# Signs of the first head by an extra matmul instead of DMA, a new order of the first block, and the mix of some pairs in a later slot

## The chip, the cores and the metric

The kernel runs on one core of a Trainium2 chip. The metric is the time of one execution on the device in microseconds; the median of three runs of the kernel before is 281.64 us (281.24 to 282.11). A profiled execution gives a page and a trace, in which times count from the start of its span. The engines are named as in the profile: PE is TensorE (matmuls; PEld its weight loads), DVE VectorE, ACT ScalarE, POOL GpSimd, SP SyncE. SPq, ACTq and POOLq stand for an engine that issues a DMA.

## The reference

Two networks follow each other. The first is an attention in which query and key only see each other when the signs of six projections agree:

```python
q_bits = (np.einsum('bhsd,dk->bhsk', q, proj) > 0).astype(np.int64)
k_bits = (np.einsum('bhsd,dk->bhsk', k, proj) > 0).astype(np.int64)
q_bucket = np.sum(q_bits * powers, axis=-1)      # k_bucket likewise
mask = q_bucket[:, :, :, None] == k_bucket[:, :, None, :]
scores = np.where(mask, scale * np.matmul(q, k.transpose(0, 1, 3, 2)), -1000000000.0)
attn = softmax(scores)
out = np.matmul(attn, v)                         # (4, 8, 768, 64)
```

Its heads side by side are x (4, 768, 512) of the second, a channel mix, where x_prev is x shifted by one position of the sequence:

```python
xk = mu_k * x + (1.0 - mu_k) * x_prev
xr = mu_r * x + (1.0 - mu_r) * x_prev
k = np.maximum(xk @ w_k, 0.0)                    # 512 -> 1024
v = k * k @ w_v                                  # 1024 -> 512
r = 1.0 / (1.0 + np.exp(-(xr @ w_r)))
return r * v
```

There are 4 batches, 8 heads of 64 columns, 768 positions.

## The kernel before

Work goes by **pairs** of heads: 16 pairs, four to a batch, numbered n; the head within a pair is j. One pair has 12 **slots**, one for each head and each block of 128 keys (jc). The loop over all 192 slots (G) writes out the order of every engine by hand; engines work through their own queues in that order and wait for each other by semaphores.

In one slot: `score` (L319) multiplies a block of keys with all queries into one of two PSUM buffers (tag `sc`), and ScalarE takes the exponential (L332). Two slots later `pv` (L340) multiplies the result with the values into `oo`, one PSUM bank for the head. After a head's last block VectorE takes reciprocals (`rc`, L363) and writes the scaled head to `ob` (L364). For pairs 0 to 3 the two heads of a pair use banks A and C in turn; from pair 4 on both use bank A, since C and D then serve the channel mix.

What a pair needs beforehand:

- `load_qk`, `load_v`: loads of q, k and v, on SP, for the first pairs on GpSimd's queue as well.
- `turn` (L263): three transposes on TensorE turn q or k of one head; VectorE copies the result out of PSUM (`tq` L272, `tk` L274) and casts one half to bfloat16 into `aq` or `ak` (L278), GpSimd casts the other half (L277).
- `bits` (L281): the signs. A matmul with the projection (L287), a comparison on VectorE that gives +0.5 or -0.5 (`sg`, L291), and for each head and side two DMAs (L297), which put the six sign rows below the 64 rows of `aq` and `ak`. A score is then one matmul over 70 rows: equal signs add 1.5, and the exponential with its scale of 256 and bias of -384 makes everything else vanish.
- `values` (L302): the values and their sums in bfloat16, all on GpSimd.

After a pair, in slot 3 of the next, `turn_out` (L371) transposes `ob` back and writes `xt`, x of the second network. The first 127 columns, x_prev across a boundary, are copied by GpSimd (L384), for the last pair of a batch by VectorE. In slot 4 `mix` (L389) subtracts (`df`, L394), multiplies (L398) and adds (L405) on VectorE: this is xk. A second part gives xr later, in slot 8 as a rule.

The matmuls of the channel mix of a batch (`kp`, `rp`, `vp`, all recorded at L424) start in slot 5 of the next batch's first pair, spread evenly over four pairs in a queue of small items. `kr` and `k` are the squared relu (L447 on ScalarE or L449 on VectorE, L455 on VectorE).

Weights come during the first pairs: `load_w` by GpSimd's queue, `load_wv` (L542) by SP into one of two staging buffers, which GpSimd casts eight slots after the issue (L550); `weights` (L587) names the slots. The DMAs that SP issues take turns on eight semaphores, so an issue waits until the one eight places ahead has landed.

Before the loop the kernel does all of pair 0's turns and signs and half of pair 1's turns.

Of the kernel before, what the change touches and what calls it, by code (L numbers as in the profile page):

```python
# [9 lines left out]
FP32 = mybir.dt.float32  # L10
BF16 = mybir.dt.bfloat16
INT32 = mybir.dt.int32
AF = mybir.ActivationFunctionType
ALU = mybir.AluOpType
AX = mybir.AxisListType

P = 128
# [12 lines left out]
def kernel(  # L30
# [13 lines left out]
    nc = tc.nc  # L44
# [123 lines left out]
    def fast():  # L168
        with ExitStack() as fx:
# [12 lines left out]
            obp = pool("ob", 2)  # L182
            rcp = pool("rc", 4)
            xtp = pool("xt", 1)
            stg = pool("stg", 2)
            aug = pool("aug", 1)
            dfp = pool("df", 1)
            mixp = pool("mix", 2)
# [74 lines left out]
            def turn(n, i, j, which):  # L263
                side = "qk"[i]
                au = augs[n % NSET]
                tp = bank(which, [P, HALF], FP32, f"tp{side}{n}_{j}")
                for c in range(3):
                    cols = slice(c * P, (c + 1) * P)
                    nc.tensor.transpose(tp[:, cols], nats[n][:, i, j, cols], ident32)  # L269
                dst = t32p.tile([P, HALF], FP32, name=f"t{side}{n}_{j}", tag=f"t{side}{j}")  # L270
                if side == "q":
                    nc.vector.tensor_copy(dst, tp)  # L272
                else:
                    nc.vector.tensor_scalar(  # L274
                        out=dst, in0=tp, scalar1=ALPHA, scalar2=None, op0=ALU.mult
                    )
                nc.gpsimd.tensor_copy(au[side, j][0:D, 0:HALF], dst[0:D, :])  # L277
                nc.vector.tensor_copy(au[side, j][0:D, HALF:S], dst[D:P, :])  # L278
                t32s[n, side, j] = dst

            def bits(n, js, which, two_queues=False):  # L281
                au = augs[n % NSET]
                groups = [(side, j) for j in js for side in "qk"]
                ng = len(groups)
                bb = bank(which, [32 * ng, HALF], FP32, f"bb{n}_{js[0]}")
                for g, key in enumerate(groups):
                    nc.tensor.matmul(  # L287
                        bb[32 * g : 32 * g + 32, :], projp, t32s[(n,) + key], start=True, stop=True
                    )
                sg = sgp.tile([32 * ng, HALF], BF16, name=f"sg{n}_{js[0]}", tag="sg")  # L290
                nc.vector.tensor_scalar(  # L291
                    out=sg, in0=bb, scalar1=0.0, scalar2=0.5, op0=ALU.is_gt, op1=ALU.subtract
                )
                for g, key in enumerate(groups):
                    eng = nc.scalar if two_queues and key[0] == "k" else nc.sync
                    for e in range(2):
                        eng.dma_start(  # L297
                            out=au[key][D:AUG, e * HALF : (e + 1) * HALF],
                            in_=sg[32 * g + NB * e : 32 * g + NB * e + NB, :],
                        )  # L300

            def values(n, j):  # L302
                vf = vfs[n][:, j, :]
# [15 lines left out]
            def score(n, j, jc):  # L319
                au = augs[n % NSET]  # L320
                pt = ptp.tile([P, S], BF16, name=f"pt{n}_{j}_{jc}", tag="pt")
                pts[n, j, jc] = pt
                sc = scp.tile([P, 2, 512], FP32, name=f"sc{n}_{j}_{jc}", tag="sc")
                for sp in range(2):
                    nc.tensor.matmul(  # L325
                        sc[:, sp, 0:HALF],
                        au["k", j][:, jc * P : (jc + 1) * P],
                        au["q", j][:, sp * HALF : (sp + 1) * HALF],
                        start=True,
                        stop=True,  # L330
                    )
                nc.scalar.activation(  # L332
                    pt.rearrange("p (s q) -> p s q", s=2),
                    sc[:, :, 0:HALF],
                    AF.Exp,
                    bias=expb,
                    scale=SCALE,
                )
# [203 lines left out]
            def load_wv(c0):  # L542
                st = stg.tile([P, 2, DM], FP32, name=f"wvs{c0}", tag="stg")
                nc.sync.dma_start(
                    out=st,
                    in_=moe_w_v[c0 * P : (c0 + 2) * P, :].rearrange("(c p) f -> p c f", p=P),
                )
                later(
                    8,
                    lambda: nc.gpsimd.tensor_scalar(  # L550
                        out=wv_sb[:, c0 : c0 + 2, :], in0=st, scalar1=0.5, scalar2=1.0,
                        op0=ALU.mult, op1=ALU.mult,
                    ),
                )
# [9 lines left out]
            for _ in range(22):  # L564
                nc.tensor.matmul(idle, epsm, epsm, start=True, stop=True)
            turn(0, 0, 0, "B")
            turn(0, 1, 0, "D")
            bits(0, (0,), "A", two_queues=True)
            load_qk(2, eng=nc.gpsimd)
            turn(0, 0, 1, "B")  # L570
            turn(0, 1, 1, "D")
            bits(0, (1,), "C")
            load_v(1)
            nc.sync.dma_start(
                out=mu_rows[0:NDC, :], in_=moe_mu_k.rearrange("(c p) -> c p", p=P)
            )
            nc.sync.dma_start(
                out=mu_rows[NDC : 2 * NDC, :], in_=moe_mu_r.rearrange("(c p) -> c p", p=P)
            )
            values(0, 0)  # L580
            turn(1, 0, 0, "B")
            turn(1, 1, 0, "D")
            values(0, 1)

            weights = {  # L587
# [3 lines left out]
            }  # L591
            LAG = 2
            MIXSLOT = 6
# [11 lines left out]
            for G in range(nslots + LAG):  # L605
                clock[0] = G
                n, s = divmod(G, 12)
                live = G < nslots
                run_due()

                if live and s == (5 if n == 0 else 3):
                    if n + 3 < NPAIRS:
                        load_qk(n + 3)
                    if n + 2 < NPAIRS:
                        load_v(n + 2)
                w = weights.get(n, {}).get(s)
                if w:
                    if w[0] == "v":
                        load_wv(w[1])
                    else:  # L620
                        load_w(*w)
                old = chunks[G - LAG] if G >= LAG else None
                first = old is not None and old[2] == 0
                if live:
                    score(*chunks[G])
                if old and not first:
                    pv(*old, oo_bank(*old[:2]))
                rate = 25.9 / (NPB * 12 + (3 if n >= NPAIRS - NPB else 0))
                ffn(rate / 2)
                mb = misc_bank(n, s)  # L630
                if live:
                    if n == 0:
                        if s in (0, 1):
                            turn(1, s, 1, "BD"[s])
                    if n == 1 and s == 0:
                        mups = bank(mb, [P, 2 * NDC], FP32, "mups")
                        nc.tensor.transpose(mups, mu_rows, ident32[0 : 2 * NDC, 0 : 2 * NDC])
                        nc.vector.tensor_copy(mu_sb, mups)
                    if s == (3 if n == 0 else 1) and n + 1 < NPAIRS:
                        bits(n + 1, (0, 1), mb)  # L640
                    if s == 3 and n >= 1:
                        turn_out(n - 1, mb)
                    if s == 4 and n >= 1:
                        mix((n - 1) // NPB, (n - 1) % NPB, 0)

                    if n in (NPB, NPB + 1) and G - NPB * 12 in (7, 9, 11, 13):
                        mix(0, (G - NPB * 12 - 7) // 2, 1)
                    if n > NPB and s == 8:
                        mix((n - 1) // NPB, (n - 1) % NPB, 1)
                    if s in (5, 7, 9, 11) and n + 2 < NPAIRS:  # L650
                        x = (s - 5) // 2
                        turn(n + 2, x % 2, x // 2, mb)
                    if s in (6, 10) and n + 1 < NPAIRS:
                        values(n + 1, s // 10)
                    if s in (8, 10) and NKEEP <= n + 1 < NPAIRS:
                        norm(n + 1, (s - 8) // 2)
                ffn(rate / 2)
                if old and first:
                    pv(*old, oo_bank(*old[:2]))
                if live and n >= NPB and n % NPB == 0 and s == MIXSLOT - 1:  # L660
                    queue.extend(ffn_items(n // NPB - 1))
# [213 lines left out]
```

## Time and profile before

| what | value |
|---|---|
| median of three runs | 281.64 us |
| profiled execution | 281.45 us |
| its span | 279.6 us |
| TensorE busy | 262.2 us (94%) |
| ScalarE busy | 215.0 us (77%) |
| VectorE busy | 198.6 us (71%) |
| GpSimd busy | 113.3 us (41%) |
| exponentials, 192 of them | 166.5 us |
| first exponential starts | 12.94 us |

The page's chain of work that ended last is followed back from the last instruction: each step is what the next one waited for. In a timeline, a line has the start, the length (of a merged group: from first start to last end), engine, line of the kernel, operation, and output and input by name; what stands in brackets is how long the engine stood idle before it and what it waited for.

### The profile page before, as it was taken

How to read it: one execution, taken by the hardware profiler on the slowest of the kernel's cores; microseconds unless marked ns; L12 is line 12 of the kernel's file. 1: busy time of each engine (PE TensorE's matmuls, PEld its weight loads, DVE VectorE, ACT ScalarE, POOL GpSimd, SP SyncE). 2: the span in 40 equal slices, each digit the busy share in tenths (PEclk: the TensorE clock that was granted, in tenths of full speed). 3: DMA queues.
4: the chain of work that ended last, by engine and by line, in shares of the span. 5: the costliest groups of instructions: out<-in, count | busy, mean ns of one | idle time of the engine just before them, and what ended most of it. 6: DMA issues, size and time to landing. Idle time of an engine off the chain costs nothing.

```text
span 279.6 us, 6894 instructions
## 1 busy us (share of the span) xinstructions
PE 262.2 (94%) x2530; PEld 165.4 (59%) x2561; DVE 198.6 (71%) x438; ACT 215.0 (77%) x318; POOL 113.3 (41%) x300
## 2 busy tenths in 40 slices
PE   7999997899999999999999999999999889989991
PEld 5466765666565665656565765656565556545540
DVE  3766839879997866769698766769698835576541
ACT  2199995898799896878989896878998898449800
POOL 5885667665554350714455260715444600000000
PEclk9999997999999999999999999999999999999997
DMA  7459597253213050726122040815220001320042
GB/s 231 167 115 208 179 328 248 43 173 101 77 59 117 6 172 4 218 110 191 59 69 108 14 164 7 272 53 166 84 60 4 5 2 39 114 76 2 0 151 86
DMA packets 19896, 29.95 MB, mean 107 GB/s; under 512 B 2184, under 2 KB 15056, under 8 KB 19856
## 3 DMA queue, kind: packets, MB, share of 16 engines
q1 hardware_dynamic: 17928, 25.89, 27.9%
q0 software_dynamic: 1536, 3.15, 5.3%
q8 instruction: 22, 0.36, 0.5%
q10 hardware_dynamic: 392, 0.40, 0.5%
q14 instruction: 18, 0.15, 0.2%
HBM read 24.12 MB, written 6.29 MB: 109 GB/s over the span
## 4 chain that ended last, share of the span: by engine, by line
PE 66%; ACT 9%; DVE 8%; DMA 7%; issue 3%; SPq 3%; POOL 2%; ACTq 0%; DVEq 0%
PE sc L325 15%; PE vp L424 13%; PE kp L424 12%; PE oo L352 8%; ACT pt L332 6%; PE rp L424 5%; DMA wvs<-in_moe_w_v_dram 4%; PE bb L287 4%; PE tpq L269 3%; PE tpk L269 2%; SPq L297 2%; PE ot L378 2%; ACT sq L256 2%; PE oo L343 1%; DMA aq<-sg 1%
## 5 line engine op out<-in xcount | busy, mean ns | idle before, releaser
L332 ACT ACTIVATE pt<-sc,expb 128x768 bf16<-128x768 f32 x192 | 166.5, 904 | 39.4 <-PE sc L325 38.1
L325 PE MATMUL sc<-aq,ak 70*128 70x384 bf16 x384 | 94.9, 328 | 3.2 <-ACT pt L332 0.8
L352 PEld LDWEIGHTS <-pt 128*128 128x128 bf16 x1152 | 61.1, 98 | 26.6 <-issue 0.8
L352 PE MATMUL oo<-va,pt 128*128 128x65 bf16 x1152 | 66.9, 194 | 0.0
L424 PE MATMUL kp<-xk,wk_sb 128*128 128x384 bf16 x256 | 57.7, 325 | 0.8 <-DVE os L487 0.8
L325 PEld LDWEIGHTS <-ak 70*128 70x128 bf16 x384 | 34.9, 98 | 29.3 <-issue 9.1
L424 PE MATMUL vp<-wv_sb,k 128*128 128x512 bf16 (+1 forms) x186 | 50.3, 370 | 0.4 <-issue 0.2
L277 POOL CAST aq<-tq 64x384 bf16<-64x384 f32 x32 | 21.1, 658 | 63.3 <-DVE tq L272 63.3
L455 DVE TENSOR_TENSOR k<-kr 128x384 bf16<-128x384 bf16 x64 | 29.0, 459 | 15.5 <-ACT kr L447 14.3
L424 PEld LDWEIGHTS <-wk_sb 128*128 128x128 bf16 x256 | 22.2, 97 | 13.3 <-issue 4.2
L256 ACT ACTIVATE sq<-qk 128x768 bf16<-128x768 f32 x32 | 27.1, 847 | 0.1
L424 PE MATMUL rp<-wr_sb,xr 128*128 128x512 bf16 x79 | 24.9, 379 | 1.2 <-DVE kr L449 0.8
L424 PEld LDWEIGHTS <-k 128*128 128x128 bf16 x200 | 17.5, 97 | 12.0 <-issue 2.7
L447 ACT ACTIVATE kr<-kp 128x384 bf16<-128x384 f32 x36 | 17.7, 491 | 7.4 <-PE kp L424 7.4
L487 DVE SCALAR_TENSOR_TENSOR os<-th,vp 128x512 f32<-128x512 bf16 (+1 forms) x25 | 16.5, 663 | 9.0 <-PE vp L424 8.9
L384 POOL COPY xt<-xt 128x127 bf16<-128x127 bf16 x12 | 3.6, 302 | 46.4 <-DVE xt L379 46.4
L311 POOL TENSOR_TENSOR s<-vf 128x192 f32<-128x192 f32 x32 | 20.8, 650 | 0.0
L277 POOL CAST ak<-tk 64x384 bf16<-64x384 f32 x32 | 19.3, 602 | 2.4 <-DVE tk L274 2.4
L274 DVE TENSOR_SCALAR tk<-tpk 128x384 f32<-128x384 f32 x32 | 17.6, 550 | 3.4 <-PE tpk L269 3.3
L272 DVE COPY tq<-tpq 128x384 f32<-128x384 f32 x32 | 17.7, 552 | 2.1 <-PE tpq L269 2.0
L269 PE MATMUL tpq<-ident,qk 128*128 128x128 f32 x96 | 16.9, 287 | 2.4 <-DVE tq L272 1.7
L379 DVE COPY xt<-ot 128x768 bf16<-128x768 bf16 x16 | 8.9, 558 | 14.3 <-PE ot L378 14.2
(60 smaller groups left out, 320.0 us busy)
## 6 DMA issues: line engine op xcount, KB each, us to landing
vf<-in_v_dram SPq DMA_DIRECT2D x16, 384.0 KB
out_dram<-os SPq DMA_DIRECT2D x23, 256.0 KB
qk<-in_q_dram SPq DMA_DIRECT2D x13, 384.0 KB
qk<-in_k_dram SPq DMA_DIRECT2D x13, 384.0 KB
wvs<-in_moe_w_v_dram SPq DMA_DIRECT2D x4, 512.0 KB
aq<-sg SPq DMA_DIRECT2D x64, 4.5 KB
wk_sb<-in_moe_w_k_dram POOLq DMA_DIRECT2D x2, 512.0 KB, 5.4
ak<-sg SPq DMA_DIRECT2D x62, 4.5 KB
```

The costliest lines, as they stand in the source:

```text
L256: nc.scalar.activation(junk, nats[n][:, i].rearrange("p j f -> p (j f)"), AF.Square, accum_out=nrm[:, i, n : n + 1],)
L269: nc.tensor.transpose(tp[:, cols], nats[n][:, i, j, cols], ident32)
L272: nc.vector.tensor_copy(dst, tp)
L274: nc.vector.tensor_scalar(out=dst, in0=tp, scalar1=ALPHA, scalar2=None, op0=ALU.mult)
L277: nc.gpsimd.tensor_copy(au[side, j][0:D, 0:HALF], dst[0:D, :])
L311: nc.gpsimd.tensor_add(s3, vf[:, 0 : 3 * D], vf[:, 3 * D : 6 * D])
L325: nc.tensor.matmul(sc[:, sp, 0:HALF], au["k", j][:, jc * P : (jc + 1) * P], au["q", j][:, sp * HALF : (sp + 1) * HALF], start=True, stop=True,
L332: nc.scalar.activation(pt.rearrange("p (s q) -> p s q", s=2), sc[:, :, 0:HALF], AF.Exp, bias=expb, scale=SCALE,)
L352: nc.tensor.matmul(oo[:, ic, :], pts[n, j, jc][:, ic * P : (ic + 1) * P], vas[n, j][:, jc, :], start=False, stop=(jc == NC_ - 1 and ic == ...
L424: nc.tensor.matmul(box["t"], lhs(), rhs(), start=(i == 0), stop=(i == len(mms) - 1))
L447: nc.scalar.activation(kr, kp, AF.Relu)
L455: 1, lambda: nc.vector.tensor_tensor(out=k2, in0=kr, in1=kr, op=ALU.mult)
```

## The change

The first head's signs (pair 0, j = 0) no longer go into the sign rows of `aq` and `ak`. `first_signs` projects each half of its q and k by a matmul of 64 rows, compares, and leaves six rows of signs at partition 0. For this head a score is two matmuls that add up in PSUM: one over 64 rows of `ak` and `aq`, one over six rows of signs.

The order of the first block is another: before the loop stand the first head's turns and signs, its values, the load of pair 2 and head 1's q. Head 1's k and signs, its values, `load_v(1)`, the mu rows and all four turns of pair 1 move into slots 0 to 3; pair 1's signs move from slot 3 to slot 4, the loads of pair 3 from slot 5 to 6, and pair 2's turns to slots 7, 9, 10 and 11. The DMAs with head 1's k signs are issued by GpSimd.

There is one staging buffer instead of two, the cast follows ten slots after the load, and the slots of the weight loads change. `mix` for xk goes from slot 4 to slot 6, save after the last pair of a batch.

```diff
-            stg = pool("stg", 2)
+            stg = pool("stg", 1)
...
-                    eng = nc.scalar if two_queues and key[0] == "k" else nc.sync
+                    eng = nc.gpsimd if two_queues and key[0] == "k" else nc.sync
...
+            def first_signs():
+
+                res = []
+                for side in "qk":
+                    bb = scp.tile([NB, 2, 512], FP32, name=f"fb{side}", tag="sc")
+                    for e in range(2):
+                        nc.tensor.matmul(
+                            bb[:, e, 0:HALF],
+                            projp[e * D : (e + 1) * D, e * NB : (e + 1) * NB],
+                            t32s[0, side, 0][e * D : (e + 1) * D, :],
+                            start=True,
+                            stop=True,
+                        )
+                    sg = consts.tile([NB, 2, HALF], BF16, name=f"fs{side}")
+                    for es in (slice(0, 2),) if side == "q" else (slice(0, 1), slice(1, 2)):
+                        nc.vector.tensor_scalar(
+                            out=sg[:, es, :], in0=bb[:, es, 0:HALF], scalar1=0.0, scalar2=0.5,
+                            op0=ALU.is_gt, op1=ALU.subtract,
+                        )
+                    res.append(sg)
+                return res
...
+                own = n == 0 and j == 0
+                rows = slice(0, D if own else AUG)
                 for sp in range(2):
                     nc.tensor.matmul(
                         sc[:, sp, 0:HALF],
-                        au["k", j][:, jc * P : (jc + 1) * P],
-                        au["q", j][:, sp * HALF : (sp + 1) * HALF],
+                        au["k", j][rows, jc * P : (jc + 1) * P],
+                        au["q", j][rows, sp * HALF : (sp + 1) * HALF],
                         start=True,
-                        stop=True,
+                        stop=not own,
                     )
+                if own:
+                    sq, sk = (x.rearrange("p e q -> p (e q)") for x in signs0)
+                    for sp in range(2):
+                        nc.tensor.matmul(
+                            sc[:, sp, 0:HALF],
+                            sk[:, jc * P : (jc + 1) * P],
+                            sq[:, sp * HALF : (sp + 1) * HALF],
+                            start=False,
+                            stop=True,
+                        )
...
-                    8,
+                    10,
                     lambda: nc.gpsimd.tensor_scalar(
...
-            bits(0, (0,), "A", two_queues=True)
+            signs0 = first_signs()
+            values(0, 0)
             load_qk(2, eng=nc.gpsimd)
             turn(0, 0, 1, "B")
-            turn(0, 1, 1, "D")
-            bits(0, (1,), "C")
...
-            values(0, 0)
-            turn(1, 0, 0, "B")
-            turn(1, 1, 0, "D")
-            values(0, 1)
...
-                1: {0: ("v", 0), 2: ("v", 2), 10: ("r", 0, 2)},
-                2: {0: ("v", 4), 2: ("v", 6), 10: ("r", 2, 2)},
+                1: {0: ("v", 0), 6: ("r", 0, 2), 10: ("v", 2)},
+                2: {4: ("r", 2, 2), 8: ("v", 4)},
+                3: {6: ("v", 6)},
...
-                if live and s == (5 if n == 0 else 3):
+                if live and s == (6 if n == 0 else 3):
...
-                        if s in (0, 1):
-                            turn(1, s, 1, "BD"[s])
+                        if s == 0:
+                            turn(0, 1, 1, "D")
+                        if s == 1:
+                            bits(0, (1,), "C", two_queues=True)
+                            values(0, 1)
+                            load_v(1)
...
+                            turn(1, 0, 0, "B")
+                        if s == 2:
+                            turn(1, 1, 0, "D")
+                        if s == 3:
+                            turn(1, 0, 1, "B")
+                            turn(1, 1, 1, "D")
...
-                    if s == (3 if n == 0 else 1) and n + 1 < NPAIRS:
+                    if s == (4 if n == 0 else 1) and n + 1 < NPAIRS:
                         bits(n + 1, (0, 1), mb)
...
-                    if s == 4 and n >= 1:
+                    if n >= 1 and s == (4 if n % NPB == 0 else 6):
                         mix((n - 1) // NPB, (n - 1) % NPB, 0)
...
-                    if s in (5, 7, 9, 11) and n + 2 < NPAIRS:
-                        x = (s - 5) // 2
-                        turn(n + 2, x % 2, x // 2, mb)
+                    ts = (7, 9, 10, 11) if n == 0 else (5, 7, 9, 11)
+                    if s in ts and n + 2 < NPAIRS:
+                        x = ts.index(s)
+                        turn(n + 2, x % 2, x // 2, "BD"[x % 2] if n < NPB else mb)
```

More of the change, by code (lines that the diff above doesn't have):

```diff
@@ L567, in fast @@
             turn(0, 1, 0, "D")
-            bits(0, (0,), "A", two_queues=True)
+            signs0 = first_signs()
+            values(0, 0)
             load_qk(2, eng=nc.gpsimd)
             turn(0, 0, 1, "B")
-            turn(0, 1, 1, "D")
-            bits(0, (1,), "C")
[L573 to L579, printed above, removed]
-            values(0, 0)
-            turn(1, 0, 0, "B")
-            turn(1, 1, 0, "D")
-            values(0, 1)
             weights = {
                 0: {2: ("k", 0, 2), 8: ("k", 2, 2)},
[2 rows of a table removed]
[3 rows of a table added]
             }
@@ L632, in fast @@
                     if n == 0:
-                        if s in (0, 1):
-                            turn(1, s, 1, "BD"[s])
+                        if s == 0:
[4 more added lines that the diff above has]
+                            load_v(1)
+                            for i, mu in enumerate((moe_mu_k, moe_mu_r)):
+                                nc.sync.dma_start(
+                                    out=mu_rows[i * NDC : (i + 1) * NDC, :],
+                                    in_=mu.rearrange("(c p) -> c p", p=P),
+                                )
+                            turn(1, 0, 0, "B")
[4 more added lines that the diff above has]
+                            turn(1, 1, 1, "D")
                     if n == 1 and s == 0:
```

## The prediction

> **What bounds the kernel now.** I read the page first, then the chain of work that ended last for the first 62 us, the timelines of single engines there, and last the timeline of one pair in the stretch where the second network's matmuls run.
>
> ```profile
> PE 262.2 (94%) x2530; PEld 165.4 (59%) x2561; DVE 198.6 (71%) x438; ACT 215.0 (77%) x318; POOL 113.3 (41%) x300
> ...
> PE 66%; ACT 9%; DVE 8%; DMA 7%; issue 3%; SPq 3%; POOL 2%; ACTq 0%; DVEq 0%
> ```
>
> TensorE is the bound over the whole, but not in the first 62 us, where no channel-mix matmul runs yet: there ScalarE's exponentials follow each other at 0.79 us (eight in 6.47 us) and TensorE has little slack. The chain there:
>
> ```profile
> 8.55 3.81 DMA aq<-sg
> ...
> 12.41 0.49 PE sc L325 x2
> ...
> 32.70 4.00 DMA wvs<-in_moe_w_v_dram
> ...
> 36.78 1.04 POOL wv_sb L550
> ...
> 40.96 0.24 POOL xt L384
> ...
> 41.23 0.57 DVE df L394
> ```
>
> The first score waits for the first head's signs, which travel by DMA from 8.55 to 12.36. Later GpSimd stands in front of a weight that has not landed, so its shift of `xt` comes at 40.96 and VectorE, whose next instruction is the mix, stands 3.52 us. TensorE then waits for `tq`, queued behind that mix, and its granted clock falls:
>
> ```profile
> 43.36 0.55 PE L269 MATMUL tpq<-ident,qk 128*128 128x128 f32 x3 [1.75 <-DVE tq L272]
> ```
>
> ```profile
> 43.40:47.40 4.00, 4.00 (x32) 2.95 (x33) 3.77 (x9) 2.24 (x3) 3.84 (x9) 0.59 0.99 320
> ```
>
> The numbers before the last two are the granted clock (0.59) and, after it, DMA share and GB/s. From pair 4 on, one pair takes about 15.5 us and TensorE is dense. What matters there is bank A, which holds `oo` of both heads in turn: the second head's first `oo` matmul (L343) can't start before `ob` of the first has been read out by VectorE. Pair 5:
>
> ```profile
> 77.88 0.56 DVE L394 TENSOR_TENSOR df<-xt 128x768 bf16<-128x768 bf16 x1 [0.18 <-POOL xt L384]
> ...
> 78.72 0.49 PE L269 MATMUL tpq<-ident,qk 128*128 128x128 f32 x3
> ...
> 79.40 0.55 DVE L272 COPY tq<-tpq 128x384 f32<-128x384 f32 x1
> ...
> 80.27 0.55 DVE L449 TENSOR_SCALAR kr<-kp 128x384 bf16<-128x384 f32 x1
> ...
> 81.66 0.56 DVE L364 TENSOR_TENSOR ob<-oo,rc 128x384 bf16<-128x384 f32 x1
> ...
> 82.73 0.33 PE L343 MATMUL oo<-vs,epsm 128*128 128x390 bf16 x1
> ```
>
> The reader is to see two things: the mix (77.88 to 79.40) fills time in which VectorE has nothing else, since `tpq` ends at 79.21; and `ob` ends at 82.22, 0.5 us before TensorE needs the bank. In pair 13 there is no margin at all:
>
> ```profile
> 207.70 0.33 PE L343 MATMUL oo<-vs,epsm 128*128 128x390 bf16 x1 [0.21 <-DVE ob L364]
> ```
>
> **Part 1, the first block.** Removed: four DMAs for the first head's signs (two on SP, two on ACT; ACT was idle there). Added: four small fp32 matmuls, one 6x768 and two 6x384 comparisons, and two more matmuls of 384 columns in each of slots 0 to 5. Moved behind the first score: the turns of head 1's k and of pair 1, and head 1's signs; before, all but two of these turns lay in the shadow of the DMA.
>
> Walk. `tq` is ready at 5.54. A pass of 384 fp32 columns costs 0.64 cold (the bb matmul of 5.60). The two halves sit in different row groups; side by side, q takes 5.60 to 6.88 and k to 8.16. That row groups run side by side isn't in the trace; four column groups do (L287 at 15.28 to 15.30). In series it would cost 2.56 us more cold, about 1.65 since the clock is full from 10. The turn of head 1's q follows, 8.3 to 8.95. VectorE's comparisons cost 0.55 per 384 columns (L291), 768 columns between 0.56 (L379) and 1.1; either is done by 8.25, and k's first by 8.95. So the first score starts at 9.0 and its exponential at about 10.35 instead of 12.94.
>
> From 9.0 to the score of slot 6 TensorE has: score pair of slot 0, cold 0.64; its signs 0.33; five scores with signs at 0.66, 3.3; five turns at 0.33, 1.65; two signs groups at 0.75, 1.5; one opening of `oo` and four groups of pv, 0.95; and 18 changes of tile shape (128 rows, 64, 32, back).
>
> ```profile
> 15.30 0.51 PE L287 MATMUL bb<-tk,projp 128*32 128x384 f32 x1
> ...
> 15.65 0.49 PE L287 MATMUL bb<-tk,projp 128*32 128x384 f32 x1
> ...
> 16.07 0.50 PE L325 MATMUL sc<-aq,ak 70*128 70x384 bf16 x2
> ```
>
> The only change of shape in the trace is at L287: the second pass starts at 15.65 and takes 0.33 (15.30 to 15.63), the score follows at 16.07, so 0.09 is left. I take 0.1, together 1.8; the ends are 0 and 0.16 (a 384-column record lasts 0.33 and they start 0.165 apart), together 2.9. Sum 10.2: slot 6 at 19.2, its exponential, after that of slot 5 at 19.15, at 19.95. Before it was at 18.19 (16.61 plus two of 0.79). So the early start is used up by six slots of about 1.5 us on TensorE: +1.75, I take +1.6 (some passes overlap). Ends: 0 (no cost of switching, then ScalarE bounds) and +3.3 (row groups in series).
>
> The Trainium skill speaks against this part: "TensorEngine Tiling (Array Packing)", section Key Properties, has a change of tiling mode drain the engine. The trace shows 0.09 at L287, less than a full drain; with a drain of 0.16 at all 18 the sum would be about 1.1 us worse.
>
> Covers: head 1's q signs stay on SP, k signs take two issues on GpSimd (0.72 each by L238) behind `values(0,0)` (2.0), which waits for v (landed by 9.1 at the latest: issue 1.67, longest landing 7.4), `load_qk(2)` (1.45) and two casts (1.3): issued by about 15.2, landed 3.8 later by 8.55 to 12.36, 19.0 against slot 6 at 19.2. `load_qk(2)` goes out 4 us later; 6.2 to landing gives 18.7 against its turn in slot 7 at 20. Pair 1's signs go out at 18.3 instead of 16.2, eight SP issues of 0.7, as before about six us ahead of slot 12. `load_v(1)` and the two mu rows follow two SP issues; they have 5 us and more. Pair 2's turns move to slots 7, 9, 10 and 11, two slots ahead of their signs. Pair 3's loads go out behind pair 1's signs, at 24.5 instead of 22.48; its first turn, in slot 17, comes at about 28.8 (28.14 before), so the thinnest cover shrinks from 5.7 to 4.3. If one cover fails it costs 1 to 2, inside the upper end.
>
> **Part 2, pairs 1 to 4.** Weights are loaded further apart, cast ten slots after their issue, and the mix moves to slot 6, two slots behind GpSimd's shift. From slot 12 (23.27) to slot 53 (62.46 starts its exponential) lie 39.2 us where 40 exponentials need 31.6. Of the 7.6 left, four signs groups keep 0.55 each. The mix of pair 1 (0.48 at 28.7) and the great stall with its cold clock (42.47 to 51.6: 1.86 + 0.76 + 0.5 + 0.67 idle, less one signs group, plus 0.4 in slower exponentials) go: 0.5 + 3.5 = 4.0. The two wr loads (0.77 of GpSimd each) move up by 4 and 6 slots; their first matmul is at 76.67. Ends -3.0 and -4.4 (the rest is spread in hundredths). What is late next is the signs group. The one stage buffer makes SP wait for GpSimd's cast, with the next pair's eight sign DMAs behind it; they are needed 11 slots (9 us) later, which hides a cast that is up to 3 us late.
>
> **Part 3, pairs 5 and up.** VectorE's order in the built program is now xt, k, tq, aq, kr, df, xk, xk, k, rc, ob. `tq` can't start before 79.25 in pair 5. Start to start: tq 0.59, aq until kp is there (80.27), kr 0.57, df 0.59, xk 0.46, xk 0.47, k 0.4, rc 0.22, ob 0.56: 83.5 against 82.22 before, and the `oo` matmul goes from 82.73 to 83.7. Same working, with each pair's own tpq and kp: pair 6 +1.0 (tpq 94.70, oo was 98.21), 9 +0.8 (kr goes ahead of tq; oo was 145.61), 13 +0.75, 14 +0.8 (it has no turns; the two k and kr come first), 10 about 0 (no kr in between). Pairs 7, 11 and 15 have no kr and k there: 3.2 of VectorE in 3.6, no wait. 4, 8, 12 keep slot 4. Sum +4.3. The waits of VectorE for GpSimd go too:
>
> ```profile
> DVE df L394 <- POOL xt L384: 6.9, 10, 3.5
> ```
>
> That is 6.9 us in ten waits; the two of pairs 1 and 2 (0.39 and 3.52) lie in part 2, the eight here are 3.0 in all, and I count nothing for them, since they lie ahead of `tpq`'s end and TensorE waited for none of them. Ends +2.0 (half of the stalls fall on waits that are there anyway, like the 0.21 above) and +5.5.
>
> **Sum.** +1.6 - 4.0 + 4.3 = +1.9 on the profiled execution's 281.45 (span 279.6 and 1.85 around it): 283.4; the median of the runs is 281.64, 0.2 above that execution, which changes nothing.
>
> **Rivals.**
> First, faster: the stalls at bank A don't come, because the margin of 0.15 to 0.8 widens as VectorE no longer stands. Only parts 1 and 2 are left: -2.4, 279.0; with a third of part 3, 280.4. It decides where `ob` ends less than 0.3 after TensorE reaches L343. For it: the eight waits that vanish. Against: that idle time can't be used later.
> Second, the first block is worse: row groups in series or the clock up one window later; +3.3 instead of +1.6, 285.1. For it: sums on TensorE leave no slack. Against: column groups overlap.
> Third, the change doesn't remove the great stall: the cast still waits for its weight, now behind one buffer and SP's queue; part 2 is -1.0, 286.4. For it: the loads of 24.17 took 7.8 to land. Against: ten slots are over 8 us.
>
> **How the numbers follow.** Forecast 0.5, first rival 0.24, second 0.18, third 0.08. The low ends together give 279.05, the high ends 287.25; cutting a tenth on each side leaves 279.6 to 286.4. About 0.3% (0.85 us) is what a measurement tells from no change. Faster than 280.8: most of the first rival, 0.22; within: the upper edge of it and the lower edge of the forecast, 0.11; slower: 0.67.
>
> **What would show it.** The first exponential at about 10.4 and slot 6's at about 20; ScalarE waiting between slots 0 and 5. No wait of VectorE's df for GpSimd's shift of `xt`, and no stretch of low clock near 44. In pairs 5, 6, 9, 13 and 14 the `oo` matmul released by VectorE's `ob` after waits of 0.6 to 1.0. Wrong if slot 6 is at or before 18.2, or if those waits are missing.

## The result and the profile after

The changed kernel takes 290.58 us in the median (288.85 to 297.14) against 281.88 for the kernel before beside it: a ratio of 1.0292, with a 95% interval of 1.0242 to 1.0342. The forecast was 283.4, with a range of 279.6 to 286.4. The profiled execution took 290.43, its span is 288.5 (279.6 before). The lines of the code have moved: from the score on, a line of the kernel before stands about 34 further down (L343 is L377, L364 is L398, L394 is L428).

The page of the changed kernel, its sums and the chain of work that ended last, shares by engine:

```profile
PE 263.2 (91%) x2546; PEld 163.6 (57%) x2577; DVE 204.0 (71%) x440; ACT 217.1 (75%) x318; POOL 120.2 (42%) x302
...
PE 57%; DVE 19%; ACT 8%; POOL 4%; issue 4%; DMA 4%; SPq 1%; DVEq 0%; ACTq 0%
```

TensorE has about the same work as before, in a span nine us longer, and VectorE's share of the chain has gone from 8% to 19%. VectorE is busy 5.4 us longer (198.6 before) and GpSimd 6.9 (113.3 before), though each has only two instructions more: something there takes longer. Two lines of its waits (total, times, longest):

```profile
ACT pt L366 <- PE sc L359: 10.0, 6, 5.0
...
PE oo L377 <- DVE ob L398: 8.6, 8, 1.6
```

The first line is ScalarE waiting for the scores of the first head. The second is the wait at bank A, which stood at 0.2 before. The waits of VectorE's `df` for GpSimd's `xt`, 6.9 us before, are gone from the list. So is the stretch of low clock: the same window as before, with the granted clock as the number before the last two:

```profile
43.40:47.40 4.00, 3.65 (x36) 1.87 (x34) 3.88 (x8) 3.33 (x5) 3.39 (x8) 1.00 0.69 215
```

Pair 5, which the prediction walked through on the trace of before. VectorE, and below it GpSimd and TensorE in the same microseconds:

```profile
79.96 0.56 DVE L272 COPY tq<-tpq 128x384 f32<-128x384 f32 x1 [1.62 <-PE tpq L269]
80.55 0.35 DVE L278 CAST aq<-tq 64x384 bf16<-64x384 f32 x1
80.89 0.56 DVE L483 TENSOR_SCALAR kr<-kp 128x384 bf16<-128x384 f32 x1
81.48 1.26 DVE L428 TENSOR_TENSOR df<-xt 128x768 bf16<-128x768 bf16 x1
82.77 0.42 DVE L432 TENSOR_SCALAR xk<-df,mu_sb 128x768 bf16<-128x768 bf16 x1
83.23 0.56 DVE L439 TENSOR_TENSOR xk<-xk,xt 128x768 bf16<-128x768 bf16 x1
...
84.19 0.56 DVE L398 TENSOR_TENSOR ob<-oo,rc 128x384 bf16<-128x384 f32 x1
```

```profile
81.23 0.50 POOL L327 CAST va<-vf 128x384 bf16<-128x384 f32 x1
...
81.73 0.58 POOL L333 TENSOR_TENSOR s<-vf 128x192 f32<-128x192 f32 x1
82.40 0.52 POOL L334 TENSOR_TENSOR s<-s 128x64 f32<-128x64 f32 x1
82.99 0.38 POOL L336 TENSOR_TENSOR vs<-s 128x64 bf16<-128x64 f32 x1
```

```profile
84.90 0.33 PE L377 MATMUL oo<-vs,epsm 128*128 128x390 bf16 x1 [1.37 <-DVE ob L398]
```

The order is as forecast. What is not is `df`: 1.26 where the same instruction took 0.56 before. The mix (`df`, `xk`, `xk`) now lies beside GpSimd's `values` of the next pair, issued in slot 6 like itself, where before GpSimd stood idle beside it in pair 5. From the start of `df` to the end of the second `xk` the mix took 1.61 us before, with no GpSimd work beside it, in 15 of 16 cases. After, where it moved, it takes 2.06 to 2.31 in pairs 5 to 14 with 1.8 to 2.2 us of GpSimd beside it, and 3.29 in pair 3, where GpSimd also casts a weight beside it.

Where the time went, cut at starts of exponentials (slot 0 of pairs 1, 5 and 15, then to the end of the span), together with the profiles of the experiments below:

| kernel | to pair 1 | pairs 1 to 4 | pairs 5 to 14 | rest |
|---|---|---|---|---|
| before | 23.27 | 47.75 | 157.54 | 51.0 |
| after | 24.11 | 47.55 | 165.42 | 51.4 |
| e2_mix_alone | 24.99 | 46.92 | 165.57 | 51.3 |
| e1_mix4 | 24.28 | 44.61 | 157.53 | 51.4 |
| e10_mix6_late_pairs | 23.92 | 44.96 | 165.27 | 51.2 |
| e7_values4 | 23.85 | 47.80 | 157.79 | 51.4 |
| e9_mix6_values4 | 23.23 | 48.30 | 161.55 | 51.2 |
| e4_mix7 | 24.09 | 46.05 | 161.09 | 51.2 |
| e5_weights_alone | 23.01 | 44.91 | 157.58 | 51.4 |
| e6_first_alone | 24.21 | 48.90 | 157.56 | 51.0 |

Some runs, nearly all of them of kernels with the new first block, stood 3 to 9 us above the others; the ratios leave them out, and the profiles of e3_values8 and e8_mix4_again, which fell on such runs, are not in the table.

### The profile page after: what moved, and what is told of

Read it like the earlier page. It is cut to its first block, busy times and chain, and to the rows that moved or that the text cites. A ratio compares the mean times of both kernels' runs of the same rounds, so it can differ in the third digit from the quotient of the medians.

```text
span 288.5 us, 6929 instructions
## 1 busy us (share of the span) xinstructions
PE 263.2 (91%) x2546; PEld 163.6 (57%) x2577; DVE 204.0 (71%) x440; ACT 217.1 (75%) x318; POOL 120.2 (42%) x302
## 4 chain that ended last, share of the span: by engine, by line
PE 57%; DVE 19%; ACT 8%; POOL 4%; issue 4%; DMA 4%; SPq 1%; DVEq 0%; ACTq 0%
PE sc L349 13%; PE vp L458 12%; PE kp L458 10%; PE oo L386 7%; ACT pt L366 6%; PE rp L458 4%; DMA vf<-in_v_dram 4%; PE bb L287 3%; DVE df L428 3%; DVE xk L439 2%; DVE xk L432 2%; DVE tq L272 2%; PE tpq L269 2%; DVE ob L398 2%; PE oo L377 2%
## 5 line engine op out<-in xcount | busy, mean ns | idle before, releaser
L349 PE MATMUL sc<-aq,ak 70*128 70x384 bf16 (+1 forms) x384 | 93.9, 325 | 1.9 <-ACT pt L366 0.5
L386 PEld LDWEIGHTS <-pt 128*128 128x128 bf16 x1152 | 60.3, 97 | 26.1 <-issue 1.0
L349 PEld LDWEIGHTS <-ak 70*128 70x128 bf16 (+1 forms) x384 | 34.4, 98 | 27.4 <-issue 7.7
L489 DVE TENSOR_TENSOR k<-kr 128x384 bf16<-128x384 bf16 x64 | 27.0, 426 | 17.3 <-ACT kr L481 16.3
L333 POOL TENSOR_TENSOR s<-vf 128x192 f32<-128x192 f32 x32 | 21.6, 674 | 0.0
L327 POOL CAST va<-vf 128x384 bf16<-128x384 f32 x32 | 18.5, 578 | 2.7 <-DMA vf<-in_v_dram 2.7
```

What stands on the lines that cost most here:

```text
L327: nc.gpsimd.tensor_copy(va[:, :, 0:D].rearrange("p (e c) d -> p e c d", e=2), vf.rearrange("p (c e d) -> p e c d", e=2, d=D),)
L333: nc.gpsimd.tensor_add(s3, vf[:, 0 : 3 * D], vf[:, 3 * D : 6 * D])
L349: nc.tensor.matmul(sc[:, sp, 0:HALF], au["k", j][rows, jc * P : (jc + 1) * P], au["q", j][rows, sp * HALF : (sp + 1) * HALF], start=True, ...
L386: nc.tensor.matmul(oo[:, ic, :], pts[n, j, jc][:, ic * P : (ic + 1) * P], vas[n, j][:, jc, :], start=False, stop=(jc == NC_ - 1 and ic == ...
L489: 1, lambda: nc.vector.tensor_tensor(out=k2, in0=kr, in1=kr, op=ALU.mult)
```

## The experiments

**The moved mix alone, and all but the moved mix.** The first kernel is the one before with this edit only:

```diff
-                    if s == 4 and n >= 1:
+                    if n >= 1 and s == (4 if n % NPB == 0 else 6):
```

> The kernel before with one edit: the mix for xk in slot 6 after pairs that GpSimd shifts. Theory S: pairs 5 to 14 lose 7.9 as in the changed kernel; the great stall near 42 us goes or shrinks (up to -3), so 285 to 290. Rival W: 283 or less, L377's counterpart (L343) waits for ob under 2 us in all.

Measured: 290.38 (288.37 to 290.68), ratio 1.0223, interval 1.0141 to 1.0305. Pairs 5 to 14 take 8.0 us longer than before, as in the changed kernel (7.9), and TensorE's wait at bank A comes back in full:

```profile
PE oo L343 <- DVE ob L364: 8.5, 8, 1.5
```

The second is the changed kernel with the opposite edit, the mix in slot 4 in all pairs.

> The changed kernel with the mix for xk back in slot 4 after every pair; first block and weights as changed. Theory S (the loss is the mix in slot 6: it stands ahead of rc and ob on VectorE, and bank A's second head waits): the eight waits of L377 for ob, 8.6 us, go but for 0.3, pairs 5 to 14 take as long as before the change (7.9 us less), the wait in front of pairs 3 and 4 goes too; 280 to 282.5. Rival W (late weights or the first block slow the later pairs): 288 or more, and the waits of L377 stay.

Measured: 279.67 and 280.55, and twice 7 us more (286.68, 287.53); in the profile of the first, pairs 5 to 14 are back at 157.53. It was run again with more rounds:

> The changed kernel with the mix back in slot 4 in all pairs, as e1_mix4, once more with more rounds, since two of the four times of e1_mix4 stood 7 us above the other two. Theory: 279.5 to 281, faster than before by 0.5 to 1%. Rival (the low times of e1_mix4 were two lucky ones and the version as a whole is not faster): a median of 282 or more.

Measured: 280.46, ratio 0.9911, interval 0.9882 to 0.9941. So the moved mix alone makes the whole loss, and the rest of the change is a gain of 0.9%.

**Which pairs.** The changed kernel with slot 4 in pairs 1 to 4 only:

```diff
-                    if n >= 1 and s == (4 if n % NPB == 0 else 6):
+                    if n >= 1 and s == (4 if n < NPB or n % NPB == 0 else 6):
```

> The changed kernel with the mix back in slot 4 in pairs 1 to 4 only; pairs 5 and up keep slot 6. Theory (the moved mix costs in both stretches): pair 4 starts at about 55 as in e1_mix4 instead of 57.5, the stretch behind it as in the changed kernel; time 287 to 288.5, 2 to 3.5 below the changed kernel. Rival (the moved mix only costs behind pair 4, where bank A is shared, and what is late at pair 4 is made up for later): within 0.5 of the changed kernel, 289.5 to 291. The forecast's own split, in which the move gains in pairs 1 to 4: slower than the changed kernel.

Measured: 288.62, ratio 1.0231 (1.0187 to 1.0274); pairs 1 to 4 take 44.96 instead of 47.55, pairs 5 to 14 165.27. The interval reaches over that of the changed kernel, so it is the stretches that tell the two apart. In the changed kernel the moved mix costs 2.6 us in the first stretch and 7.7 in the second, against 157.53 with the mix in slot 4. In the early pairs the banks are not shared; there the lateness shows at the turns. With the weights of before the first stretch is another matter: in e2_mix_alone it takes 46.92, 0.8 less than before. So in pairs 1 to 4 the parts of the change do not add up.

**Is it GpSimd that makes the mix longer, and does that cost time?** The kernel before, the mix in its old place, with GpSimd's work brought beside it from pair 4 on:

```diff
-                    if s in (6, 10) and n + 1 < NPAIRS:
+                    if s in ((6, 10) if n < 4 else (4, 10)) and n + 1 < NPAIRS:
                         values(n + 1, s // 10)
```

> The kernel before, with nothing of the change: only GpSimd's values of the next pair's first head (a cast of 128x384, a subtraction chain and small writes, about 2.2 us) go from slot 6 to slot 4 from pair 4 on, where they run beside VectorE's mix, which keeps its place. Theory (VectorE's bfloat16 instructions take longer while GpSimd works): the mix, 1.61 us before with GpSimd idle beside it, takes 2.0 to 2.4 in pairs 5 to 15 with about 2 us of GpSimd beside it; tq, kr and ob follow 0.4 to 0.7 later, so that waits of 0.1 to 0.5 at bank A appear where the margin was small; time +1 to +4, 283 to 286. Rival (the mix took longer in slot 6 because of what lies around it on VectorE, not because of GpSimd): the mix stays at 1.61 and the time within 0.5 of the kernel before.

Measured: 282.69, ratio 1.0018 (0.9994 to 1.0042). Pair 5:

```profile
78.51 0.82 DVE L394 TENSOR_TENSOR df<-xt 128x768 bf16<-128x768 bf16 x1 [0.18 <-POOL xt L384]
79.37 0.63 DVE L398 TENSOR_SCALAR xk<-df,mu_sb 128x768 bf16<-128x768 bf16 x1
80.04 0.56 DVE L405 TENSOR_TENSOR xk<-xk,xt 128x768 bf16<-128x768 bf16 x1
80.53 0.54 DVE L272 COPY tq<-tpq 128x384 f32<-128x384 f32 x1
```

The reader is to see `df` at 0.82 instead of 0.56, the first `xk` at 0.63 instead of 0.42. The mix takes 2.09 in most pairs where GpSimd now runs beside it (1.99 in one), against 1.61: the theory is right about the cause. It is wrong about the price: pairs 5 to 14 are 0.25 longer in all. In slot 4 VectorE then has nothing else to do until `tpq` is there, and the 0.5 us are absorbed, while in slot 6 `k`, `rc` and `ob` are queued behind the mix, and TensorE behind `ob`.

**The order alone.** Since `values` in slot 4 costs next to nothing there (0.25), the same edit takes GpSimd out of the way of the moved mix. This kernel is e2_mix_alone with `values` in slot 4 wherever the mix is in slot 6; VectorE's order is the same in both.

```diff
-                    if s in (6, 10) and n + 1 < NPAIRS:
+                    if s in ((4, 10) if n % NPB else (6, 10)) and n + 1 < NPAIRS:
```

> The kernel before with the mix of pairs moved as in e2_mix_alone, and GpSimd's values of the next pair's first head from slot 6 to slot 4 in the same pairs, where e7_values4 showed that they cost nothing. VectorE's order is that of e2_mix_alone, GpSimd is out of the mix's way. Theory (order and the slower mix both count): the mix back at 1.6 to 1.8, each pair with a stall at bank A 0.4 to 0.7 shorter, time 284 to 287, so 3 to 6 below e2_mix_alone. Rival (the order alone makes the whole loss; a longer mix costs nothing, as in e7_values4): 289 to 291, with the waits at bank A as in e2_mix_alone (8.5 us).

Measured: 284.57, ratio 1.0086 (1.0058 to 1.0113). Pair 5, VectorE and then TensorE, and the wait at bank A over the whole:

```profile
81.35 0.56 DVE L394 TENSOR_TENSOR df<-xt 128x768 bf16<-128x768 bf16 x1
81.94 0.42 DVE L398 TENSOR_SCALAR xk<-df,mu_sb 128x768 bf16<-128x768 bf16 x1
82.40 0.56 DVE L405 TENSOR_TENSOR xk<-xk,xt 128x768 bf16<-128x768 bf16 x1
...
83.36 0.56 DVE L364 TENSOR_TENSOR ob<-oo,rc 128x384 bf16<-128x384 f32 x1
...
84.07 0.33 PE L343 MATMUL oo<-vs,epsm 128*128 128x390 bf16 x1 [0.67 <-DVE ob L364]
```

```profile
PE oo L343 <- DVE ob L364: 4.2, 5, 1.3
```

`df` is back at 0.56, and TensorE's wait at the bank is 0.67 instead of 1.37. The wait is halved in all (8.5 to 4.2), and so is the loss in pairs 5 to 14: 8.0 with GpSimd beside the mix, 4.0 without. In three of these pairs, 7, 10 and 11, 0.33 of GpSimd is still beside the mix, which takes 1.8 there, and in pair 14 the mix takes 2.12 beside 1.96 of GpSimd (2.09 in the kernel before). So the slower mix makes about half of the loss, and VectorE's order about the other half, of which 3.1 lie in pairs 5, 6, 9 and 13, where nothing of GpSimd is left beside the mix.

The same was tried earlier from the other side, in the changed kernel, with `values` of the first head in slot 8 instead of 6 from pair 4 on.

> The changed kernel; from pair 4 on the first head's values of the next pair are made in slot 8 instead of slot 6, so that GpSimd has only its 0.69 us cast beside the mix. Theory P (the mix is 1.6 us alone and 2.3 us beside GpSimd, and this is the half of the loss that the prediction lacked): the mix of pairs 5 to 14 falls to 1.6 to 1.9, the waits of L377 fall from 8.6 to 4 to 5.5, 286 to 287.5. Rival O (the order on VectorE alone costs it): mix or not, within 1 us of the changed kernel, 289.5 to 291.

Measured: a median of 290.48, of 289.3 in the runs that the ratio counts; ratio 1.0227 (1.014 to 1.0313). In pairs 5 to 13 of its profile the moved mix is at 1.59 to 1.79, and in 14 at 2.12; TensorE's wait at bank A is 4.1 in five, as in e9_mix6_values4, and pairs 5 to 14 take 162.3 us, 3.1 less than in the changed kernel. So mix and waits are those of theory P. The time of the whole is above what it said, and its interval reaches over that of the changed kernel: it does not show the gain firmly.

**One slot later still.** The changed kernel with 7 for the 6 in the rule of the mix:

> The changed kernel with the mix in slot 7 instead of 6, so that rc and ob of the first head stand ahead of it on VectorE. Theory S with bank A as the place: the waits of L377 for ob are under 1.5 us in all, and 282 to 285 (what is late then is tk and the turns behind it, up to 0.5 a pair). Rival L (VectorE is late as a whole, whatever stands first): PE waits of the same size show up at turns and kr, 288 or more.

Measured: 285.32, ratio 1.0104 (1.0078 to 1.013). This is just above what theory S allowed. No wait at bank A is left; pairs 5 to 14 still take 3.5 longer than before, with six waits of `tpq`'s matmuls for VectorE's `tk` (2.0 in all, and 3.8 of the weight loads ahead of them). VectorE is late as such: with the mix behind `ob`, what stands behind the mix waits, and that is the turns.

**The other two parts, each alone.** The kernel before with the weight part only:

```diff
-            stg = pool("stg", 2)
+            stg = pool("stg", 1)
...
-                    8,
+                    10,
...
-                1: {0: ("v", 0), 2: ("v", 2), 10: ("r", 0, 2)},
-                2: {0: ("v", 4), 2: ("v", 6), 10: ("r", 2, 2)},
+                1: {0: ("v", 0), 6: ("r", 0, 2), 10: ("v", 2)},
+                2: {4: ("r", 2, 2), 8: ("v", 4)},
+                3: {6: ("v", 6)},
```

> The kernel before with only the weight part of the change: one staging buffer, casts ten slots after the load, new slots of the weight loads. First block as before, the mix in slot 4 everywhere. Theory (the three parts are nearly additive, and the moved mix alone cost the 8 to 9 us): the stall at 42 to 44 with its low clock goes, the first exponential stays at 12.9 and slot 6 at 18.2; from slot 12 to slot 53 about 36 us where there were 39.2; time 278.5 to 280. Rival (the gain seen with the mix put back came from the first block, and the weights do nothing without it, because the second cast still waits for its load): a wait of 2 or more behind GpSimd's shift of xt in pair 2 stays, time 281.5 to 282.5. The forecast's part 2 as it stood, -4.0 with the mix of pair 1 kept at slot 4: 277.5 to 278.5.

Measured: 278.78 (277.67 to 278.84), ratio 0.9862, interval 0.9826 to 0.9898. This is the fastest of all kernels here, below the one before and the changed one. From slot 12 to slot 53 it takes 35.6 where there were 39.2. Behind that 0.75 is given back, in pair 4, where the fourth cast now lies beside VectorE's (second line GpSimd):

```profile
60.32 1.12 DVE L278 CAST aq<-tq 64x384 bf16<-64x384 f32 x1
...
60.19 1.05 POOL L550 TENSOR_SCALAR wv_sb<-wvs 128x1024 bf16<-128x1024 f32 x1 [2.27 <-DMA wvs<-in_moe_w_v_dram]
```

The 64x384 cast takes 0.35 elsewhere. The kernel before with the first block only:

> The kernel before with only the first block of the change: signs of the first head by matmul, the new order of turns, values and loads, pair 2's turns in slots 7, 9, 10, 11. Weights and mix as before. (The six-row signs borrow two buffers of the output tiles, since with two staging buffers there is no room of their own.) Theory: first exponential at 8.9, slot 6 at 19.2, slot 12 at 24.1, so +0.8 to +1.0 there; the great stall of pair 2 follows the landing of its weights, so part of this delay is lost in it; time 281.5 to 283. Forecast's part 1 as it stood: +1.6, 283 to 283.5. Rival (the new first block is a gain by itself, because pair 2's and pair 3's turns come at better places): below 281.

Measured: 283.74, ratio 1.0042 (1.0012 to 1.0072). Slot 12 comes at 24.21, 0.94 later; in this profile the great stall is longer too (pairs 1 to 4 take 48.90 against 47.75), so the delay was not lost in it as the theory had it. The granted clock is at half for longer as well, from 45.61 to 52.44, where in the profile of before it was from 44.10 to 47.51; what share that has is not shown. By the times the first block costs 1.2 us (0.3 to 2.0).

## Why the prediction was right or wrong

The direction was right and the amount was not: +8.7 by the medians instead of +1.9. Two of the three terms failed, both at the moved mix: part 2 counted it as a gain, and part 3 priced it without its neighbour. By stretches of the profiled executions:

**Part 1, +1.6 forecast, +0.84 measured at slot 12.** The mechanism held; the size rests in part on luck. The first block of the changed kernel on TensorE, then on ScalarE:

```profile
5.80 0.81 PE L308 MATMUL fbq<-tq,projp 64*6 64x384 f32 x4 [0.57 <-DVE tq L272]
6.66 0.81 PE L308 MATMUL fbk<-tk,projp 64*6 64x384 f32 x4
...
7.90 0.48 PE L349 MATMUL sc<-aq,ak 64*128 64x384 bf16 x2
...
13.38 0.49 PE L349 MATMUL sc<-aq,ak 64*128 64x384 bf16 x2
13.81 0.49 PE L359 MATMUL sc<-fsq,fsk 6*128 6x384 bf16 x2
```

```profile
8.90 0.90 ACT L366 ACTIVATE pt<-sc,expb 128x768 bf16<-128x768 f32 x1 [5.01 <-PE sc L359]
10.43 0.90 ACT L366 ACTIVATE pt<-sc,expb 128x768 bf16<-128x768 f32 x1 [0.63 <-PE sc L359]
...
18.37 5.76 ACT L366 ACTIVATE pt<-sc,expb 128x768 bf16<-128x768 f32 x7 [1.30 <-PE sc L359]
```

The last line is slot 5 and six more. The two halves of a side do lie side by side: 0.81 for both, where four passes of 0.33 in series would take 1.3. The walk had the passes at 0.64, so 1.28 for each side; the first score came at 7.90, not 9.0. The 0.64 was read rightly from the trace of before, where TensorE's work is slower up to about 10 us (a group of two passes there, and one like it later):

```profile
5.60 1.49 PE L287 MATMUL bb<-tq,projp 128*32 128x384 f32 x2 [0.20 <-DVE tq L272]
...
10.28 0.83 PE L287 MATMUL bb<-tk,projp 128*32 128x384 f32 x2
```

The trace's record of the granted clock begins at 9.96 there, and at 4.62 in the changed kernel's. Ahead of its first record the views show 1.00, which is then not a measurement. In e3_values8, the changed kernel's first block with a record only from 31.29, the walk's size comes out:

```profile
6.14 1.45 PE L308 MATMUL fbq<-tq,projp 64*6 64x384 f32 x4 [0.37 <-DVE tq L272]
7.38 1.49 PE L308 MATMUL fbk<-tk,projp 64*6 64x384 f32 x4
...
9.63 0.82 PE L349 MATMUL sc<-aq,ak 64*128 64x384 bf16 x2
```

The sides stand 1.24 apart, and the first score comes 3.49 after the first sign matmul, where the walk had 3.4 and the changed kernel's profile has 2.10. So the mis-sized term is the time at which TensorE becomes fast, carried over from one execution, and +0.84 belongs to one pair of executions: e5_weights_alone, with the first block of before and a record from 4.96, reaches slot 12 at 23.01, 1.1 ahead of the changed kernel, and e7_values4, with the same block and a record from 4.75, at 23.85, 0.3 ahead, with a wait of 2.16 for a load of k.

From the first score to that of slot 6 TensorE needs 10.56 (7.90 to 18.46), against 10.2 in the sum; a weight load waits 0.51 in it for head 1's k to land. A change of tile shape costs the 0.1 that was taken (0.43 from 13.38 to 13.81, less 0.33 of work), so the dearer drain of 0.16 that the prediction held against itself did not come. ScalarE waits for TensorE in slots 0 to 5, as said, and slot 6 comes at 19.17, where 19.95 was forecast. None of the covers listed failed. The second rival is out.

**Part 2, -4.0 forecast, -1.04 measured from slot 12 to slot 53.** Alone it is worth what was said: -3.6 in e5_weights_alone. The great stall went, and the third rival is out. The low clock went too, but it was hardly the price: in the profile of e7_values4, with the weights and the mix of before in these pairs, the stall is there and the granted clock is 1.00 all through it, and the stretch takes 38.91 against 39.19. What failed is that the moved mix was counted as a gain here, for a wait of 0.5. In e10_mix6_late_pairs, where it is back in slot 4 in these pairs, the same stretch takes 35.6; in the changed kernel 38.15. It brought its own stalls: VectorE, behind a mix of 2.25 beside GpSimd, is late for the turns. The trace at the signs of pair 4, VectorE, GpSimd, TensorE:

```profile
42.23 0.83 DVE L439 TENSOR_TENSOR xk<-xk,xt 128x768 bf16<-128x768 bf16 x1
...
45.10 1.16 DVE L278 CAST aq<-tq 64x384 bf16<-64x384 f32 x1
46.19 0.53 DVE L274 TENSOR_SCALAR tk<-tpk 128x384 f32<-128x384 f32 x1
...
44.95 1.04 POOL L584 TENSOR_SCALAR wv_sb<-wvs 128x1024 bf16<-128x1024 f32 x1
...
46.78 0.83 PE L287 MATMUL bb<-tk,projp 128*32 128x384 f32 x2 [0.17 <-DVE tk L274]
...
56.51 0.55 PE L269 MATMUL tpk<-ident,qk 128*128 128x128 f32 x3 [1.17 <-DVE tk L274]
```

`tk`, which the signs need, comes behind the cast of 1.16, which lies beside GpSimd's weight cast. The last line is the same one turn later: the mix of 3.29 in pair 3 lies ahead of `tk`, and the turn that needs its bank waits 1.17. Of the 2.6 us that the moved mix costs in pairs 1 to 4, 2.1 lie in pair 3. The prediction said that the signs group would be late next and put no price on it. The cast of the fourth weight in pair 4 (0.75 in e5_weights_alone) was not counted either, so that all of pairs 1 to 4 came to -0.20.

**Part 3, +4.3 forecast, +7.9 measured in pairs 5 to 14.** This is the other step that failed: "df 0.59, xk 0.46, xk 0.47" are start-to-start times from a place where GpSimd stood idle, carried to a place where it works. With most of that excluded, as in e9_mix6_values4, the walk through VectorE's order held: the waits at bank A stand in just the five pairs that it named, 0.65 to 0.88 in 5, 6, 9 and 13 and 1.29 in 14 (forecast 0.6 to 1.0). By pair it measured +0.62 in 5, +1.04 in 6, +0.78 in 9, +0.66 in 13 (forecast 0.95, 1.0, 0.8, 0.75), nothing in 14 (forecast 0.8), and 0.25 to 0.46 in 7, 10 and 11 (forecast 0), which still have 0.33 of GpSimd beside the mix. That the sum, +4.0, comes so near 4.3 is thus partly luck. The longer mix adds the rest: in the changed kernel 5, 6, 9 and 13 are up by 1.3 to 1.5, and 7, 10 and 11, where a wait of 0.6 at the bank now comes as well, by 0.7 to 1.0. Pairs 8 and 12, whose mix had not moved, are unchanged to 0.01.

The price was to be seen in the trace of before, in the one late pair that has `values` beside the mix. VectorE and GpSimd at 218:

```profile
218.17 0.83 DVE L394 TENSOR_TENSOR df<-xt 128x768 bf16<-128x768 bf16 x1 [0.39 <-POOL xt L384]
219.03 0.63 DVE L398 TENSOR_SCALAR xk<-df,mu_sb 128x768 bf16<-128x768 bf16 x1
219.70 0.56 DVE L405 TENSOR_TENSOR xk<-xk,xt 128x768 bf16<-128x768 bf16 x1
```

```profile
218.08 0.51 POOL L305 CAST va<-vf 128x384 bf16<-128x384 f32 x1
...
218.59 0.86 POOL L311 TENSOR_TENSOR s<-vf 128x192 f32<-128x192 f32 x1
219.53 0.32 POOL L312 TENSOR_TENSOR s<-s 128x64 f32<-128x64 f32 x1
```

That is 2.09 for the mix. The prediction read GpSimd's queue for what it delivers late, not for what lies beside VectorE's instructions once they are moved. The Trainium skill has the rule, in "SBUF — State Buffer", section Who interferes with whom: a VectorE instruction with two inputs in SBUF contends with a GpSimd instruction that reads SBUF, and whoever comes first keeps the shared ports for its whole instruction. The trace agrees in kind for `df` and the adding `xk` (0.56 to as much as 1.26 and 0.83 in pairs 5 to 14); the size has to be taken from rows.

**The sum.** In place of +1.6 - 4.0 + 4.3 the changed kernel has +0.84, -0.20 for pairs 1 to 4, +7.9, and 0.4 at the end: 8.9, the difference of the spans. The 0.4 is not the change's: e7_values4, whose end is that of before, has it too. Of the 7.0 between this and the forecast +1.9, 3.8 come from part 2 and 3.6 from part 3; part 1 takes 0.8 off. The first rival (no stalls at bank A) is out: they came eight times, up to 1.6, where 0.6 to 1.0 in five pairs was forecast.

## What to carry to other kernels

A duration belongs to the place where it was measured: before moving an instruction, lay the other engine's timeline over its new place, and price it by a row that has the same neighbour (here 2.09 at 218 against 1.61 elsewhere). Slack decides what such a lengthening costs: 0.4 to 0.5 us a pair in front of an engine that waits anyway cost 0.25 us over ten pairs, while 0.45 to 0.7 in front of `ob` cost 4.0. Prices of parts need not add up: in pairs 1 to 4 the moved mix gains 0.8 with the old weights and costs 2.6 with the new ones. A change of several parts is worth taking apart even when its direction is clear: the weight part alone takes 1.4% off the time, under a sum that adds 2.9%.

## What the runs showed of the hardware

That VectorE's bfloat16 instructions of 128x768 slow down beside GpSimd was not in the prediction: the three of the mix take 1.61 us with GpSimd idle, 1.99 to 2.09 with `values` beside them in slot 4 and 2.06 to 2.31 in slot 6 of pairs 5 to 14. A cast with one input is touched too: 64x384 from float32 takes 0.35, and 1.12 to 1.16 beside a GpSimd cast of 128x1024; in the trace of before, at 46.85, it takes 3.06 beside two of these, a smaller cast and the issue of a DMA in a row on GpSimd (46.52 to 49.76). GpSimd pays as well: 0.52 for the 128x64 sum in pair 5 that takes 0.32 elsewhere. Two fp32 matmuls of 64 rows in different halves of the array overlap (0.81 for both, four passes). TensorE starts slow, for a time that differs from execution to execution; it ends at the first record of the granted clock (4.62 us in the changed kernel's profile, 9.96 in that of before, 12.88 in e2_mix_alone, 31.29 in e3_values8). Ahead of it a group of two passes of 384 fp32 columns takes 1.45 to 1.49 in the last three of these, and behind it such groups take 0.81 to 0.83.
